# A long convolution beside a gated feed-forward layer: one outer transform table for all residues, phase factors in the inner tables

## The chip, the cores and the metric

The kernel runs on one core of one Trainium2 chip. The metric is the time on the device in microseconds (us). A core has a matrix engine (TensorE; PE in the profile, PEld for its weight loads), VectorE (DVE), ScalarE (ACT), GpSimd (POOL) and SyncE (SP), which here issues nearly all DMAs. The engines run beside one another and wait for each other through semaphores.

## What is computed

With S = 2048 positions and D = 640 channels, bf16 in and out:

```python
xn = layernorm(A_q)                                  # over D, no scale, no shift
k_shift[s] = sum_m A_k[s - m] * shift_k[:, m]        # 4 taps
kv = k_shift * A_v
y = irfft(rfft(kv, 4096) * rfft(ssm_k, 4096))[:2048] + kv * ssm_D   # causal convolution, length 2048
h = sigmoid(xn @ w_gate) * (xn @ w_up)               # 640 -> 1728
out = A_q + xn * y + h @ w_down                      # 1728 -> 640
```

## The kernel before

Position s is written 16 p + b, with p the partition (0 to 127) and b the residue (0 to 15); all activations lie in SBUF as [p, b, channel]. Two streams of work share the engines.

The **feed-forward stream** goes through four groups t of 512 positions. xnT holds the transposed xn of a group. For each of 13 column blocks fc of 128, `product` (L284 to L290) makes five matmuls of 128x512 for the gate and five for the up weights; `gate_ev` puts the gate through a sigmoid on ScalarE (L297) and `up_ev` multiplies on VectorE (L303); a fourteenth block (L309) holds the last 64 columns of both. `down_mm` (L332) then makes for each of four position blocks two halves of 320 columns out of 14 matmuls each, in two parts of seven, and `down_ev` (L337) adds them to x.

The **convolution stream** goes through five chunks c of 128 channels. `kv_op` builds kv on VectorE (L365 to L374), and `h_turn` (L351) brings in the filter, so that `kvh` holds kv and the filter side by side. The transform has 128 frequency rows k1 (real and imaginary part) times 16 inner frequencies. It has four steps on PE:

- `st1_mm` (L391, L393): the outer transform over p. For each residue b and each half (cosine, sine) one 128x128 table of S1 is the stationary operand, with 128 columns of kv and 128 of the filter as moving operands. S1 has 32 such tables, because the phase of residue b is in it. A block n has four residues, that is eight matmuls of 128 columns. `st1_ev` brings the block to SBUF, `wr1` (L405) writes it to a DRAM tensor d1, and `rd2` (L415) reads it back with frequency row k1 = 4 r + q split so that q, the half and the residue are on the partitions.
- `st2_mm` (L424): the inner transform over the 16 residues, as 32x32 matmuls. PE is used as 4 x 4 tiles of 32 rows and 32 columns; tile (q, g) takes the data of rows q and two values of r at a time, 512 columns, and all of them have the same weights, SM[:, 0]. A step s has 16 such matmuls; there are 20 steps. `st2_ev` brings the result to `xz`.
- `prod` (L437, L439) multiplies the two spectra on VectorE. `inv1_mm` (L453) goes back over the inner frequencies: two sets of weights (i = 0, 1, accumulated) times 16 tiles, 512 columns each, 32 matmuls for each of 10 steps y. `inv1_ev` and `wr2` (L469, L473) write to a DRAM tensor d2, and `rdb` (L483) reads it back.
- `inv2_mm` (L492): the outer transform back, with TB (again one table for each residue), eight matmuls of 128 columns for each of 20 blocks. `inv2_q` and `inv2_x` (L497, L502) multiply with xn and add to x.

The copies from PSUM that are written `copy` in these helpers run on ScalarE (recorded as L251) or on VectorE (L254).

**Order.** Nothing is scheduled automatically. Each kind of step has a letter and a list (`chains`, L560 to L668), and a string ORDER (L670) says letter by letter which list gives the next step; each engine then runs its instructions in that order. Capital F, I and J are the evictions B, A and C put on VectorE. TURNS gives the order within the loads (m) and the stores (o).

**Prologue** (L505 to L557). Position blocks 0 to 3 of x are loaded, two by SP and ACT together and two by one each; then come gate and up weights for the first 128 columns (gate by SP, up by ACT), for the next 128, and for columns 256 to 511 (SP). Thirteen matmuls on zeros (L522, `busy`) keep PE running meanwhile. The layer norm of blocks 0, 1 and 3 uses VectorE's bn_stats (L205), aggregate (L209) and variance (L238), then POOL's power (L242) and VectorE's xn (L247). That of block 2 uses two ScalarE passes over x with accumulated sums (`ln_sums`, L215 and L216), VectorE's L222, the same power, and L233. `turn(i)` transposes block i on PE (L261) and copies it to xnT on ScalarE (L264). In between, as FIRST says, `quarter` makes the products of fc 0 and 1 for one position block at a time (L279, 128 columns): g00 is the gate of fc 0 for block 0, t1 is `turn(1)`.

Of the kernel before, what the change touches and what calls it, by code (L numbers as in the profile page):

```python
# [17 lines left out]
DM = 640  # L18
# [8 lines left out]
g00 t1 u00 t2 g10 u10 t3 g01 u01 g11 u11 g02 u02 g12 u12 g03 u03 g13 u13  # L27
# [3 lines left out]
def _bf16_bits(a):  # L31
    a = np.ascontiguousarray(a, dtype=np.float32)
    u = a.view(np.uint32)
    r = (u + 0x7FFF + ((u >> 16) & 1)) & 0xFFFF0000
    return (r >> 16).astype(np.uint16)


def _tables():

    p = np.arange(P)
    k1 = p + 0.25
    s1 = np.zeros((P, NB, 2, P))
# [4 lines left out]
    tb = s1.transpose(3, 2, 1, 0) / 2048.0  # L50
    th = 2 * np.pi * np.outer(np.arange(NB), np.arange(NB)) / 16.0
    c, s = np.cos(th), np.sin(th)
    s2 = np.block([[c, -s], [s, c]])
    a1 = np.block([[c.T, s.T], [-c.T, -s.T]])
    a2 = np.block([[-s.T, c.T], [-s.T, c.T]])
    small = np.stack([s2, a1, a2], 1)
    return _bf16_bits(s1), _bf16_bits(tb), _bf16_bits(np.concatenate([small] * NQ, 0))
# [3 lines left out]
def kernel(  # L61
# [23 lines left out]
    s1bits, tbbits, smbits = _tables()  # L85
# [3 lines left out]
    SMd = nc.inline_tensor(smbits, name="tabSM")  # L89
# [16 lines left out]
    SM = SMt.bitcast(BF16)  # L106
# [111 lines left out]

    def ln_sums_var(g, i):

        d = lns[g]
        nc.vector.tensor_scalar(d["var"][:, i:i + 1], d["ss"][:, i:i + 1], 1.0 / DM, 1e-5, op0=ALU.mult, op1=ALU.add)  # L222
# [116 lines left out]
    def store(b0, b1, lo, hi):  # L339
        sync.dma_start(outr[:, b0:b1, lo:hi], x[:, b0:b1, lo:hi])  # L340
# [37 lines left out]
    def quad(i):  # L378
        return slice(32 * i, 32 * i + 32)
# [38 lines left out]
    def st2_mm(s):  # L418

        d = groups[s]  # L420
        d["ps"] = ps = [psC.tile([P, 2, 2, 2, P], F32, name="ps2", tag="c") for _ in range(2)]
        for g in range(4):
            for q in range(NQ):
                nc.tensor.matmul(ps[q // 2][quad(g), q % 2, :, :, :], lhsT=SM[quad(q), 0, :],  # L424
                                 rhs=d["t2"][quad(q), 2 * g:2 * g + 2, :], start=True, stop=True)
# [16 lines left out]
    def inv1_mm(y):  # L442

        c, y2 = divmod(y, 2)
        d = chunks[c]
        if y2 == 0:
            d["d2"] = dr.tile([32, P, P], BF16, name="d2", bufs=NC)
        d["pa", y] = ps = [psC.tile([P, 2, 512], F32, name="psa", tag="c") for _ in range(2)]
        lo, hi = sorted((2 * y % 3, (2 * y + 1) % 3))
        for i in range(2):  # L450
            for q in range(NQ):
                for g in range(4):
                    nc.tensor.matmul(ps[g // 2][quad(q), g % 2, :], lhsT=SM[quad(g), 1 + i, :],  # L453
                                     rhs=xz[quad(g), lo:hi + 1:hi - lo, 1 + i, 2 * q:2 * q + 2, :],
                                     start=(i == 0), stop=(i == 1))
# [30 lines left out]
    def inv2_mm(c, m):  # L486

        bi = chunks[c]["bi", m // 2]
        chunks[c]["pb", m] = ps = psG.tile([P, 4, P], F32, name="psb", tag="g")
        for i in range(4):  # L490
            for h in range(2):
                nc.tensor.matmul(ps[:, i, :], lhsT=TB[:, h, 4 * m + i, :], rhs=bi[:, h, 4 * (m % 2) + i, :],  # L492
                                 start=(h == 0), stop=(h == 1))
# [30 lines left out]
    def turn(i):  # L524
        xn_mm(i)
        xn_ev(i)
# [10 lines left out]
    ln_sums(0, 2)  # L537
# [42 lines left out]
    def hs(c):  # L580
        return [(load_h, c)]
# [7 lines left out]
    for k in ((load_w, sync, 512, 768, 0),  # L589
              (load_w, sync, 512, 768, 1),  # L590
              (load_taps, 0),
              (sync.dma_start, SMt[:], SMd.ap()),
# [11 lines left out]
              (sync.dma_start, S1t[:], S1d.ap()),  # L604
              *hs(1),
# [4 lines left out]
    for k in ((load_x, sync, 2), (load_x, sync, 3), (sync.dma_start, TBt[:], TBd.ap())):  # L610
        step("n", *k)
# [53 lines left out]
    for b in range(12, NB - 1):  # L665
# [5 lines left out]
    mmgmmgsummggggsmsugmmgmgLsuuLsZgLkkggskkmggmmuusggnkLsmuLugsPmkmgumgHgggsLusguggllsuggguHggummgggkmL  # L671
    mLlmDkaaTkkkluAgkkkueAeekggggktkkekkuaaHgukAmAgsawAakgAPgsuuHlmkuKgmkkkTagskkKwwauAAggDkkgKaashtukkk
    AkAggkgwmwsuslauaAAHgklgkkuVVskaaAAggaksgkkkwAaAggrbuugkkkwsuBBgpkKrHpDasATaAtkugsKnguwwbKBgKFgasgAa
    AggasuskkpkkVkahwAnrLAwLgguugkpHHgaaAkAgggDcukCJLggeealuALuaIwggbrkeBBgggeurkkkVTuukkKkubggBBgbBgBpw
    rgppkasupaAIuggstkkkukVwkWaAaAhskgugPaAarkpggAcksJCggbwsuuHHKggDBWlpgBrassupukakggpAAsbBBgggkucwkRss
    VkkCJggbBupupdqggrrqBspWsbupgguBdBcskrJCgqgbggkFRBusubgFllpBwgaAudaggaAWdarrqqgpAAlgwpppeauqRagAIuqq
    egeecJCuuggubFpBpWpggbrrggBBuudqdcCJwwgqpgsRWgqpbFBpggsuurbBBprpggssugucdJCWdgpbsgqFBgubBBpqsgpgspuc
    rCgJgspqqubgugqRdBBdrbWpqqgpgsugqqBBpcCJprsuggbsuBBRdqWpgsdRRpgggsqqucuJCgggWsqduqqdqggudquqdRRooggg
    gqoggoooqqududugqqqguqooddqqqqgggougoouooo
    """  # L680
    TURNS = {"m": [1, 7, 4, 9, 21, 0, 20, 2, 10, 5, 6, 13, 12, 14, 8, 17, 15, 11, 22, 18, 16, 19, 23, 25, 24, 3],
        "o": [2, 0, 4, 1, 5, 3, 7, 6, 8, 11, 10, 9, 12, 13]}
# [35 lines left out]
```

## Time and profile before

| | |
|---|---|
| median of 3 runs | 236.09 us (235.89 to 236.45) |
| profiled execution | 236.47 us, of which the span of its instructions is 234.5 us |
| PE clock granted | 1.00 throughout |
| matmuls and weight loads | 2201 of each |
| L288 (gate and up products) | 500 matmuls of 512 columns |
| L391, L393 (outer transform) | 320 matmuls of 128 columns |
| L492 (outer transform back) | 160 matmuls of 128 columns |
| L424, L453 (inner, 32x32) | 320 and 320 matmuls of 512 columns |
| DMA | 56.78 MB, of it S1t and TBt 1024 KB each, SMt 24 KB |

A row of the profile's table of groups gives line, engine and operation, what is written and read with the shape, how often, then busy time and mean length, and last how long the engine had stood idle before and what ended that. A row of a timeline gives start, length, engine, line, operation, shape, and in brackets the idle time before it with its cause. The end of a matmul is modelled: a 512-column matmul is recorded as 380 ns long, but the next one starts 216 ns after it, so the pace is read from starts. The waits of an engine are listed as total time, times, and the longest.

### The profile page before, as it was taken

What the parts mean: (1) busy time and instruction counts of PE and PEld (TensorE: products, weight loads), DVE (VectorE), ACT (ScalarE), POOL (GpSimd) and SP (SyncE); (2) the same over time, 40 slices, a digit from 0 to 9 for tenths busy, and PEclk for the clock granted to TensorE, in tenths of its full rate; (3) what the DMA queues carried; (4) which work ended last, traced back from release to release, by engine and by line L of the source; (5) the groups of instructions that cost most, each with busy time, mean ns of one, the idle gap of its engine ahead of it and who ended that gap; (6) DMA issues with size and microseconds to landing.
All of it is one profiled execution on the core that took longest, in us unless ns stands there. A gap on an engine that the chain in (4) does not pass through costs nothing. (4 is left out here: it accounts for less than half of the span.)

```text
span 234.5 us, 5457 instructions
## 1 busy us (share of the span) xinstructions
PE 227.0 (97%) x2201; PEld 130.8 (56%) x2201; DVE 198.5 (85%) x327; ACT 136.3 (58%) x199; POOL 12.1 (5%) x27
## 2 busy tenths in 40 slices
PE   6799999999999999999999999999999999999994
PEld 2664445777556555766554534478554435356772
DVE  4433764899999999969999999999999999998673
ACT  2737777346578696977776876564365666652000
POOL 5301020200001000003000000000000000000000
PEclk9999999999999999999999999999999999999999
DMA  6999999879959998999997997999899898376675
GB/s 168 272 283 279 290 338 226 260 141 253 313 186 232 301 309 219 309 253 295 256 230 178 280 301 185 276 254 246 188 288 294 205 268 209 115 163 197 220 240 169
DMA packets 98926, 56.78 MB, mean 242 GB/s; under 512 B 58518, under 2 KB 93142, under 8 KB 98646
## 3 DMA queue, kind: packets, MB, share of 16 engines
q1 hardware_dynamic: 97814, 55.95, 89.4%
q10 hardware_dynamic: 1088, 0.49, 0.9%
q8 instruction: 17, 0.28, 0.5%
q14 instruction: 7, 0.06, 0.1%
HBM read 36.12 MB, written 18.35 MB: 232 GB/s over the span
## 5 line engine op out<-in xcount | busy, mean ns | idle before, releaser
L288 PEld LDWEIGHTS <-w 128*128 128x128 bf16 x500 | 46.5, 98 | 54.8 <-issue 5.0
L332 PE MATMUL pd<-wd,hT 128*128 128x320 bf16 (+2 forms) x448 | 64.5, 299 | 0.0
L288 PE MATMUL pu<-xnT,w 128*128 128x512 bf16 x250 | 62.3, 380 | 0.0
L288 PE MATMUL pg<-xnT,w 128*128 128x512 bf16 x250 | 62.2, 379 | 0.0
L332 PEld LDWEIGHTS <-hT 128*128 128x128 bf16 x448 | 42.1, 98 | 18.7 <-issue 2.1
L303 DVE TENSOR_TENSOR hT<-sig,pu 128x512 bf16<-128x512 bf16 x52 | 34.7, 680 | 15.2 <-PE pu L288 11.1
L251 ACT CAST t<-ps 128x1024 bf16<-128x1024 f32 x37 | 36.0, 1013 | 18.7 <-PE ps L393 16.0
L251 ACT CAST xz<-ps 128x1024 bf16<-128x1024 f32 x34 | 33.0, 1015 | 17.8 <-PE ps L424 17.8
L297 ACT ACTIVATE sig<-pg 128x512 bf16<-128x512 f32 x52 | 30.8, 602 | 20.7 <-PE pg L288 15.1
L439 DVE TENSOR_TENSOR xz<-xz 128x2048 bf16<-128x2048 bf16 x20 | 24.3, 1216 | 0.1
L371 DVE TENSOR_TENSOR acc<-acc,tmp 128x1024 bf16<-128x1024 bf16 x30 | 20.6, 688 | 0.5
L369 DVE TENSOR_TENSOR tmp<-kx,sc 128x1024 bf16<-128x1024 bf16 x30 | 20.6, 686 | 0.5
L393 PE MATMUL ps<-kvh,S1t 128*128 128x128 bf16 x160 | 20.8, 219 | 0.0
L391 PE MATMUL ps<-kvh,S1t 128*128 128x128 bf16 x160 | 20.8, 218 | 0.0
L337 DVE TENSOR_TENSOR x<-pd,x 128x320 bf16<-128x320 f32 (+2 forms) x32 | 14.9, 481 | 5.3 <-PE pd L332 5.2
L391 PEld LDWEIGHTS <-S1t 128*128 128x128 bf16 x160 | 15.5, 97 | 2.2
L393 PEld LDWEIGHTS <-S1t 128*128 128x128 bf16 x160 | 15.4, 96 | 2.2
L497 DVE TENSOR_TENSOR yx<-psb,xn 128x512 bf16<-128x512 f32 x20 | 13.7, 686 | 1.7 <-PE psb L492 0.9
L437 DVE STREAM_SHUFFLE xz<-xz 128x512 f32<-128x512 f32 x20 | 14.5, 724 | 0.0
L251 ACT CAST ao<-psa 128x1024 bf16<-128x1024 f32 x8 | 8.1, 1012 | 8.9 <-PE psa L453 8.8
L215 ACT ACTIVATE xn<-x 128x640 bf16<-128x640 bf16 x13 | 9.5, 732 | 3.5 <-DMA x<-in_A_q_dram 3.5
L254 DVE CAST ao<-psa 128x1024 bf16<-128x1024 f32 x8 | 9.8, 1222 | 2.0 <-PE psa L453 1.9
(55 smaller groups left out, 168.4 us busy)
## 6 DMA issues: line engine op xcount, KB each, us to landing
d<-t SPq DMA_DIRECT2D x20, 512.0 KB, 4.7
t<-d SPq DMA_DIRECT2D x20, 512.0 KB, 6.1
bi<-d SPq DMA_DIRECT2D x8, 512.0 KB, 6.5
d<-ao SPq DMA_DIRECT2D x6, 512.0 KB, 6.5
kx<-in_A_k_dram SPq DMA_DIRECT2D x10, 256.0 KB, 4.9
hn<-in_A_ssm_k_dram SPq DMA_DIRECT2D x20, 128.0 KB, 4.0
kvh<-in_A_v_dram SPq DMA_DIRECT2D x10, 256.0 KB, 5.1
x<-in_A_q_dram SPq DMA_DIRECT2D x3, 640.0 KB, 7.2
```

The source lines that it names most:

```text
L251: nc.scalar.copy(out=out, in_=in_)
L288: nc.tensor.matmul(pg[:, :], lhsT=w[:, c, u * UP + fc * P:u * UP + (fc + 1) * P], rhs=xnT[:, :, c, :], start=(c == 0), stop=(c == NC - 1))
L297: nc.scalar.activation(sig[fc][:, :], pgs[0, fc][:, :], ACT.Sigmoid)
L303: nc.vector.tensor_tensor(hT[:, fc, :], sig[fc][:, :], pgs[1, fc][:, :], ALU.mult)
L332: nc.tensor.matmul(pd[:, :], lhsT=hT[:, fc, bb * P:(bb + 1) * P], rhs=wd[:, fc, es], start=(fc == 0), stop=(fc == NFC - 1))
L337: nc.vector.tensor_tensor(x[:, 4 * t + bb, es], pds[bb, half][:, :], x[:, 4 * t + bb, es], ALU.add)
L369: nc.vector.tensor_tensor(d["tmp"][:, :, :], kx[:, lo + 3 - m:hi + 3 - m, :], sb(m), ALU.mult)
L371: nc.vector.tensor_tensor(d["acc"][:, :, :], d["acc"][:, :, :], d["tmp"][:, :, :], ALU.add)
L391: nc.tensor.matmul(ps[:, i, 0:P], lhsT=S1[:, b, h, :], rhs=cin[c]["kvh"][:, 0, b, :], start=True, stop=True)
L393: nc.tensor.matmul(ps[:, i, P:2 * P], lhsT=S1[:, b, h, :], rhs=hp[:, b // 2, b % 2, :], start=True, stop=True)
L437: nc.vector.stream_shuffle(z[:, 2, :, :].bitcast(F32), z[:, 1, :, :].bitcast(F32), swap)
L439: nc.vector.tensor_tensor(z[:, 1:3, :, :], z[:, 0:1, :, :].to_broadcast((P, 2, 8, P)), z[:, 1:3, :, :], ALU.mult)
```

## The change

- **Outer tables.** S1 and TB keep only the table of residue 0 (two of 128x128 each). The phase 2 pi k1 b / 2048 of residue b, which depends on the frequency row, moves into the inner weights: FW has a 32x32 matrix for each of the 128 frequency rows (forward), IW two for each (back).
- **`st1_mm`, `inv2_mm`.** Since all residues have the same stationary operand, a block is two matmuls of 512 columns in place of eight of 128. `st1_ev` puts the result back in the old order of d1.
- **`st2_mm`, `inv1_mm`.** A frequency row has its own weights, so the moving operand is cut: a forward step has 32 matmuls of 256 columns, in two passes over the 16 tiles; a step back has 128 matmuls of 128 columns, in eight passes.
- **Prologue.** Block 2 takes its statistics on VectorE like the others. The first weights come as one load of 256 columns for the gate and one for the up weights, both by SP. FIRST has a new order.
- **Order.** ORDER and TURNS are new strings, with the same steps (S1t, FWt, IWt, TBt in place of S1t, SMt, TBt among the loads). Evictions on VectorE: six of `st2_ev` as before, seven of `st1_ev` for three, seven of `inv1_ev` for ten.
- **Last store.** The one of the last 128 columns is issued by ScalarE.

The lines of ORDER and the table functions are cut here.

```diff
-g00 t1 u00 t2 g10 u10 t3 g01 u01 g11 u11 g02 u02 g12 u12 g03 u03 g13 u13
+g00 g10 t1 u00 u10 t2 g01 g11 u01 u11 t3 g02 u02 g12 u12 g03 u03 g13 u13
...
-    S1t = res.tile([P, NB, 2, P], U16, name="S1t")
-    TBt = res.tile([P, 2, NB, P], U16, name="TBt")
-    SMt = res.tile([P, 3, 32], U16, name="SMt")
+    S1t = res.tile([P, 2, P], U16, name="S1t")
+    TBt = res.tile([P, 2, P], U16, name="TBt")
+    IWt = res.tile([P, 2, 32, 32], U16, name="IWt")
+    FWt = res.tile([P, 32, 32], U16, name="FWt")
...
-        sync.dma_start(outr[:, b0:b1, lo:hi], x[:, b0:b1, lo:hi])
+        (nc.scalar if b1 == NB and hi == DM else sync).dma_start(outr[:, b0:b1, lo:hi], x[:, b0:b1, lo:hi])
...
-        pss[n] = ps = psC.tile([P, 4, 2 * P], F32, name="ps1", tag="c")
-        for i in range(4):
-            b = 4 * n4 + i
-            nc.tensor.matmul(ps[:, i, 0:P], lhsT=S1[:, b, h, :], rhs=cin[c]["kvh"][:, 0, b, :], start=True, stop=True)
-            hp = cin[c]["kvh"][:, 1, :, :].rearrange("p b c -> p (b c)").rearrange("p (b c e) -> p b e c", b=8, e=2)
-            nc.tensor.matmul(ps[:, i, P:2 * P], lhsT=S1[:, b, h, :], rhs=hp[:, b // 2, b % 2, :], start=True, stop=True)
+        pss[n] = ps = psC.tile([P, 2, 4, P], F32, name="ps1", tag="c")
+        hp = cin[c]["kvh"][:, 1, :, :].rearrange("p b c -> p (b c)").rearrange("p (b c e) -> p b e c", b=8, e=2)
+        nc.tensor.matmul(ps[:, 0, :, :], lhsT=S1[:, h, :], rhs=cin[c]["kvh"][:, 0, 4 * n4:4 * n4 + 4, :],
+                         start=True, stop=True)
+        nc.tensor.matmul(ps[:, 1, :, :], lhsT=S1[:, h, :], rhs=hp[:, 2 * n4:2 * n4 + 2, :, :], start=True, stop=True)
...
-        copy(out=d[n // 2][:, o:o + 4, :, :].rearrange("p b s c -> p b (s c)"), in_=pss[n][:, :, :])
+        copy(out=d[n // 2][:, o:o + 4, :, :].rearrange("p b s c -> p s b c"), in_=pss[n][:, :, :, :])
...
-        for g in range(4):
-            for q in range(NQ):
-                nc.tensor.matmul(ps[q // 2][quad(g), q % 2, :, :, :], lhsT=SM[quad(q), 0, :],
-                                 rhs=d["t2"][quad(q), 2 * g:2 * g + 2, :], start=True, stop=True)
+        for e in range(2):
+            for g in range(4):
+                for q in range(NQ):
+                    nc.tensor.matmul(ps[q // 2][quad(g), q % 2, e, :, :], lhsT=FW[quad(q), 8 * (s % 4) + 2 * g + e, :],
+                                     rhs=d["t2"][quad(q), 2 * g + e, :], start=True, stop=True)
...
-        for i in range(2):
-            for q in range(NQ):
-                for g in range(4):
-                    nc.tensor.matmul(ps[g // 2][quad(q), g % 2, :], lhsT=SM[quad(g), 1 + i, :],
-                                     rhs=xz[quad(g), lo:hi + 1:hi - lo, 1 + i, 2 * q:2 * q + 2, :],
-                                     start=(i == 0), stop=(i == 1))
+        for k in range(2):
+            s = 2 * y + (k if lo == 2 * y % 3 else 1 - k)
+            for e in range(2):
+                j = 8 * (s % 4) + 4 * e
+                o = (2 * k + e) * P
+                for i in range(2):
+                    for q in range(NQ):
+                        for g in range(4):
+                            nc.tensor.matmul(ps[g // 2][quad(q), g % 2, o:o + P], lhsT=IW[quad(g), i, j + q, :],
+                                             rhs=xz[quad(g), s % 3, 1 + i, 2 * q + e, :],
+                                             start=(i == 0), stop=(i == 1))
...
-        for i in range(4):
-            for h in range(2):
-                nc.tensor.matmul(ps[:, i, :], lhsT=TB[:, h, 4 * m + i, :], rhs=bi[:, h, 4 * (m % 2) + i, :],
-                                 start=(h == 0), stop=(h == 1))
+        for h in range(2):
+            nc.tensor.matmul(ps[:, :, :], lhsT=TB[:, h, :], rhs=bi[:, h, 4 * (m % 2):4 * (m % 2) + 4, :],
+                             start=(h == 0), stop=(h == 1))
...
-        load_w((sync, nc.scalar)[u], 0, P, u)
-    for u in range(2):
-        load_w(sync, P, 256, u)
+        load_w(sync, 0, 256, u)
...
-    ln_sums(0, 2)
     ln_stats(0, 1)
     ln_xn(0, 0)
     ln_ready(0, 1)
     turn(0)
+    ln_stats(0, 2)
+    ln_xn(0, 1)
+    ln_ready(0, 2)
     ln_stats(0, 3)
-    ln_sums_var(0, 2)
-    ln_pow(0, 2, 3)
-    ln_xn(0, 1)
+    ln_xn(0, 2)
     ln_ready(0, 3)
-    ln_sums_xn(0, 2)
     ln_xn(0, 3)
...
-              (sync.dma_start, SMt[:], SMd.ap()),
...
+              (sync.dma_start, FWt[:], FWd.ap()),
...
-    for k in ((load_x, sync, 2), (load_x, sync, 3), (sync.dma_start, TBt[:], TBd.ap())):
+    for k in ((load_x, sync, 2), (load_x, sync, 3), (sync.dma_start, IWt[:], IWd.ap()),
+              (sync.dma_start, TBt[:], TBd.ap())):
```

More of the change, by code (lines that the diff above doesn't have):

```diff
@@ L49, in _tables @@
         s1[:, b, 1, :] = -np.sin(psi)
-    tb = s1.transpose(3, 2, 1, 0) / 2048.0
+    tb = s1[:, 0].transpose(2, 1, 0) / 2048.0
     th = 2 * np.pi * np.outer(np.arange(NB), np.arange(NB)) / 16.0
[L52 to L57, printed above, removed]
+    iw = np.zeros((4, 32, 2, 4, 2, NQ, 32))
+    for g in range(4):
+        for s4 in range(4):
+            for e in range(2):
+                for q in range(NQ):
+                    ph = th + 2 * np.pi * k1[4 * (8 * s4 + 2 * g + e) + q] * np.arange(NB)[None, :] / 2048.0
+                    ci, si = np.cos(ph), np.sin(ph)
+                    iw[g, :, 0, s4, e, q, :] = np.block([[ci, si], [-ci, -si]])
+                    iw[g, :, 1, s4, e, q, :] = np.block([[-si, ci], [-si, ci]])
+    fw = np.zeros((NQ, 32, 32, 32))
+    for q in range(NQ):
+        for r in range(32):
+            ph = th + 2 * np.pi * k1[4 * r + q] * np.arange(NB)[:, None] / 2048.0
+            fw[q, :, r, :] = np.block([[np.cos(ph), -np.sin(ph)], [np.sin(ph), np.cos(ph)]])
+    return (_bf16_bits(s1[:, 0]), _bf16_bits(tb), _bf16_bits(iw.reshape(P, 2, 32, 32)),
+            _bf16_bits(fw.reshape(P, 32, 32)))
 @with_exitstack
@@ L83 @@
     Drow = A_ssm_D.rearrange("(o d) -> o d", o=1)
[L85 removed]
+    s1bits, tbbits, iwbits, fwbits = _tables()
     srow = A_shift_k.rearrange("d m -> (d m)").rearrange("(o n) -> o n", o=1)
@@ L421, in st2_mm @@
         d["ps"] = ps = [psC.tile([P, 2, 2, 2, P], F32, name="ps2", tag="c") for _ in range(2)]
-        for g in range(4):
-            for q in range(NQ):
-                nc.tensor.matmul(ps[q // 2][quad(g), q % 2, :, :, :], lhsT=SM[quad(q), 0, :],
-                                 rhs=d["t2"][quad(q), 2 * g:2 * g + 2, :], start=True, stop=True)
+        for e in range(2):
+            for g in range(4):
+                for q in range(NQ):
+                    nc.tensor.matmul(ps[q // 2][quad(g), q % 2, e, :, :], lhsT=FW[quad(q), 8 * (s % 4) + 2 * g + e, :],
+                                     rhs=d["t2"][quad(q), 2 * g + e, :], start=True, stop=True)
     def st2_ev(s, n, copy=act_copy):
```

34 lines of the change are left out of this document (18 added, 16 removed).

## Prediction

> **What bounds the kernel now.** I read the page's busy shares first, then the waits of PE, then the busy time by stage, and last the timelines of the prologue, of one transform stage and of the end.
>
> ```profile
> PE 227.0 (97%) x2201; PEld 130.8 (56%) x2201; DVE 198.5 (85%) x327; ACT 136.3 (58%) x199; POOL 12.1 (5%) x27
> ```
> ```profile
> PE pg L279 <- ACT xnT L264: 1.7, 1, 1.7
> PE idle L522 <- DVE hT L120: 1.2, 1, 1.2
> PE pt L261 <- DVE xn L247: 0.7, 1, 0.7
> PE psa L453 <- DVE xz L437: 0.6, 1, 0.6
> ```
>
> The second view says more than the first: PE waits four times in all, three of them before 8.53 us, and no wait names a DMA. From 8.53 us to its last matmul at 231.2 us PE stands still for 0.57 us. So the time is the first 8.5 us, PE's own work, and the 3.2 us behind it. By stage VectorE is nearly as full: busy 39.3 of 40 us between 50 and 90 us, 37.3 between 90 and 130 and 38.7 between 130 and 170, so it has 4.7 us to spare in 120.
>
> Prologue, columns start, length, engine, line:
>
> ```profile
> 6.12 0.74 ACT L215 ACTIVATE xn<-x 128x640 bf16<-128x640 bf16 x1 [3.46 <-DMA x<-in_A_q_dram]
> ...
> 7.81 0.67 ACT L264 COPY xnT<-pt 128x640 bf16<-128x640 bf16 x1
> ```
> ```profile
> 5.69 0.45 PE L261 MATMUL pt<-ident,xn 128*128 128x128 bf16 x5 [0.69 <-DVE xn L247]
> ...
> 8.53 0.44 PE L279 MATMUL pg<-xnT,w 128*128 128x128 bf16 x5 [1.74 <-ACT xnT L264]
> ```
> ```profile
> 6.95 0.10 PEld L279 LDWEIGHTS <-w 128*128 128x128 bf16 x1 [0.65 <-DMA w<-in_B_w_gate_dram]
> ```
>
> The first transposes are done at about 6.15 us, but their copy (L264) stands behind ScalarE's two statistics passes over x (L215, L216; 6.12 to 7.9 us), so the first product starts at 8.53, though its weights were there at 6.95.
>
> Transform, the small blocks (32x32 tiles) and the 128-column blocks:
>
> ```profile
> 128.56 0.43 PE L424 MATMUL ps<-t,SMt 32*32 32x512 bf16 x16
> ```
> ```profile
> 173.17 0.65 PE L453 MATMUL psa<-xz,SMt 32*32 32x512 bf16 x32
> ```
> ```profile
> 191.99 0.20 PEld L453 LDWEIGHTS <-SMt 32*32 32x32 bf16 x31 [0.55 <-issue]
> ```
> ```profile
> 172.35 0.89 PE psb L492 x16
> ```
>
> Sixteen tile matmuls take 0.43 us and 32 take 0.65: a second round of 16 tiles adds 0.22 us, which is what one 512-column matmul of full size takes (five in 1.08 us in the chain). So the 16 tiles stream at the same time, and the rest of a block is fixed. From a block's start to the next start it is 0.58 us for 32 and 0.37 for 16, so about 0.15 us beyond the rounds. The third line is what the change hangs on: 31 weight loads of 0.088 us each start within 0.20 us, (0.20 - 0.09)/30 = 3.7 ns apart, with the first round's matmuls between them.
>
> **Part by part.** *Outer transforms (L391, L393, L492).* Forty blocks of eight 128-column matmuls and twenty of the same on the way back become blocks of two 512-column ones. The columns stay the same (1024), so only the joints go. 16 in 0.89 us is 0.445 for a block; the sixteen of L391 and L393 that run from 132.17 to 133.08 us give 0.455. Two of 512 take 2 x 0.216 = 0.432. I take 0.02 less for each of 60 blocks, **-1.0 us** (-0.8 to -1.4). The weight loads that go (480 full ones become 120) run beside matmuls and free no time by themselves.
>
> *Forward inner blocks (L424).* 16 x 512 columns become 32 x 256: two rounds of 0.11 us for one of 0.22, with the second round's loads in the shadow of the first. **0** (0 to +0.2 over 20 blocks).
>
> *Backward inner blocks (L453).* 32 matmuls of 512 columns become 128 of 128, ten times: eight rounds of 16, each with new weights. A round needs 0.056 us (the 128-column pace) and 16 issues of 3.7 ns need 0.059, so the two are level: 8 x 0.059 + 0.15 = 0.62 for 0.58, **+0.4 us** in all. No row shows more than 32 such pairs in a row, nor a tile reloaded every 0.056 us, so I bound it. Below, 8 x 0.054 + 0.15 = 0.58 makes it nothing. Above, from two rows: if a load's 0.088 us is bare in every round, 8 x 0.144 + 0.15 = 1.30, or +7.2 us in all; if pairs come only at the pace of the full-size 128-column runs (0.056 a pair), 128 x 0.056 + 0.15 = 7.3, or +67 us. I stay near the low end, because its row is the same instruction on the same tiles.
>
> The Trainium skill, TensorE: Matmul & The Clock Gate, section "Wait — 56ns, not 53.3ns?", speaks against this edit: matmuls never start closer than about 25 ns however few columns they have. By it a block would take an estimated 128 x 25 ns = 3.2 us and the ten +27 us. The row of 31 loads in 0.20 us does not bear it out across different tiles.
>
> *Prologue.* ScalarE's passes for block 2 go; VectorE does bn_stats for it. ScalarE then copies xnT at 6.2 to 6.9 us. The gate weights now come as one 256-column load, 320 KB for 160 first; by the second 160 KB load of before, which landed at about 7.6, I put its landing at 7.5, and g00 there. VectorE by the rows (statistics 0.89, aggregate, variance and their gaps 0.6, POOL power 0.56, xn 0.45): xn of block 1 starts at 7.0 (8.00 now), of block 2 at 8.6 (8.88), of block 3 at 10.0 (9.41). PE: g00 g10 to 8.1, t1 to 8.35, u00 u10 once the up weights land at about 8.7 (both up loads of before were in by 8.9), t2 and four quarters to 10.65, t3 to 10.95 (xn of block 3 is there at 10.45), eight quarters to 13.2. Now it is 13.87: **-0.65 us**. The bounds are -1.0 (20 quarters and three transposes back to back from 7.5) and 0 (weights only at 8.5). Its new bound is VectorE's third xn, 0.2 us ahead of its use.
>
> *Loads.* Tables shrink from 2072 KB (S1t, TBt, SMt) to 896 KB, and the last store goes out on ScalarE's queue. No PE wait names a DMA; the forward reads of d1 land 0.7 to 4 us ahead of their blocks and the last read of d2 2.6 us ahead, so bytes saved are worth **0**. Should that cover fail, the shortest, 0.7 us, is gone first. At the end the last addition ends at 231.55, SP issues the store at 231.83 behind another one; issued by ScalarE at about 231.6 it lands **0.2 us** earlier.
>
> *Order and evictions.* The hand-written order is new. VectorE takes 20 evictions for 19 (1.22 us each, against 1.01 on ScalarE), so 1.2 us more in a stage with 4.7 spare: **0**, and +1.2 if that spare lies elsewhere.
>
> Sum: -1.0 + 0 + 0.4 - 0.65 - 0.2 = -1.45 us. The profiled execution took 236.47 (span 234.46, 2.0 around it), so 235.0; it lies 0.4 above the median of 236.09, where the same sum gives **234.7**.
>
> **Rivals.**
> 1. *Supply of the small matmuls bounds (slower).* 128 pairs are four times the longest run shown, and each block pays if its instructions come slower than they ran from a filled queue. It decides from 4.8 ns a pair: the other terms give 1.85 us, 0.185 a block, and (0.58 + 0.185 - 0.15)/128 = 4.8. At 56 ns a pair the time is 302. For: only bursts of 32 pairs are shown, and they had piled up behind a wait. Against: no break in them. By the Trainium skill's 25 ns (same section) it would be an estimated 262. Chance 0.08.
> 2. *Bare weight loads.* Each round shows its 0.088 us: 241.5. For: 32-column loads last nearly as long as a round is now short. Against: first-round matmuls last 385 ns and those with weights already in 372, so a bare load costs 13 ns. Chance 0.10.
> 3. *The new order leaves PE waiting for VectorE*, as at 191.4 us (0.57 us for a shuffle). Three such waits, 1.5 us or so: 236.2 (235.5 to 237.5). For: VectorE at 96% from 50 to 170 us, one more eviction. Against: four waits in the whole trace of before. Chance 0.20.
> 4. *The prologue does not do what it says*: weights in one larger load arrive at 8.5, and the start does not move: 235.3. Chance 0.10.
>
> **How the numbers follow.** The forecast, 234.7 (its own range 234.1 to 235.4), has 0.52. A measurement of this kernel can tell about 0.2%, 0.47 us, so faster is below 235.6 and slower above 236.6. Faster: 0.50 of the forecast and 0.07 of rival 4, 0.57. Same: 0.02, 0.03 and 0.11 of rival 3, 0.16. Slower: 0.09 of rival 3 and rivals 1 and 2, 0.27. The range leaves out rivals 1 and 2 (0.18) and reaches over rival 3: 233.8 to 237.6.
>
> **What would show it.** Backward blocks of 128 at 0.6 us from start to next start (over 0.75 the gain is gone; 1.3 is rival 2; over 2 is rival 1); outer blocks at 0.43; first product at about 7.5 and first 512-column product at 13.2; PE without waits after that. New rows of PE waiting for VectorE, or a first product that names the weight DMA beyond 8 us, would make the forecast wrong.

## The result: 251.3 us, slower by 6.5%

| | before | after |
|---|---|---|
| median of 4 runs each, in turn | 236.2 us | 251.3 us (250.9 to 253.0) |
| after / before | | 1.065, 95% interval 1.060 to 1.070 |
| profiled execution / its span | 236.47 / 234.5 us | 252.97 / 250.8 us |
| first 512-column product starts | 13.87 us | 12.55 us |
| backward inner block, start to next start | 0.583 us | 1.198 us |
| last matmul starts | 231.00 us | 246.70 us |
| from there to the end | 3.5 us | 4.1 us |

Single executions of three kernels below ran with PE at about half of its pace (h1, 393 us) or a sixth (b128 and p, 1325 us each) from start to end; they are left out of the times, and so are the profiles taken from them (the first of h1, the only one of p).

The page of the changed kernel (busy time, granted clock by slices of 6.27 us, and the DMA queue that carries instructions):

```profile
PE 238.7 (95%) x3121; PEld 126.6 (50%) x3121; DVE 202.4 (81%) x331; ACT 134.1 (53%) x194; POOL 12.1 (5%) x27
...
PEclk9999999999999999999999999998895999999999
...
q8 instruction: 24, 0.39, 0.7%
```

PE is the bound still, with 11.7 us more of busy time, though the columns are the same; VectorE's share has fallen to 81%. The clock, 1.00 throughout before, dips in slices 27, 28 and 30 (counted from 0). The last row is of a kind that the prediction did not use: q8 moves 24 pieces of 16 KB (17 before). The trace has 6242 matmuls and weight loads of PE, 260 for each piece, and 4402 before, 259 for each: so I take these to be PE's own instructions, 256 to a piece.

PE's waits, total, times and longest:

```profile
PE ps L432 <- issue: 5.5, 2, 3.6
PE pd L340 <- issue: 1.2, 1, 1.2
PE idle L532 <- DVE hT L133: 1.2, 1, 1.2
PE pg L296 <- DVE hT L311: 0.2, 1, 0.2
```

Of the forecast's rivals, waiting for VectorE has 0.2 us. What is new is "issue": PE waits for nothing that the profile shows, three times, 6.7 us. One backward block, and the stretch around the longest of these waits (columns as before):

```profile
136.07 1.26 PE L466 MATMUL psa<-xz,IWt 32*32 32x128 bf16 x128
137.27 0.82 PE L296 MATMUL pg<-xnT,w 128*128 128x512 bf16 x3
```
```profile
184.96 0.32 PE L432 MATMUL ps<-t,FWt 32*32 32x256 bf16 x14
188.84 0.61 PE L432 MATMUL ps<-t,FWt 32*32 32x256 bf16 x18 [3.56 <-issue]
189.38 2.31 PE L296 MATMUL pu<-xnT,w 128*128 128x512 bf16 x5
191.48 1.91 PE L504 MATMUL psb<-bi,TBt 128*128 128x512 bf16 x4
```

The first fence: 1.20 us from block to product. Inside it, by the starts in the trace, the matmuls of the first 32 pairs of weight load and matmul start within 0.12 us, then none until 0.25, and from there every pair starts 8.33 ns after the one before, without any mark of the rounds of 16: 0.25 + 95 x 8.33 ns, and 0.15 from the last pair to the product, are the 1.20 us. The second fence: a forward block stops after 14 of its 32 matmuls and goes on 3.8 us later. Behind it the five matmuls of one product take 2.1 us from start to next start; at full clock five take 1.08.

The three pauses have a place in common. Counted along PE's stream (weight loads, matmuls and the 14 records of its sequencer, from 1), the first instruction behind each is record 3266, 3778 and 4290: 512 apart, that is two pieces. And each time a piece of q8 had landed 1.3 to 1.5 us before PE went on (153.14 and 154.42 us, 170.68 and 172.19, 187.43 and 188.84). So my theory after the profile: **the backward blocks run at the pace at which PE is given instructions, 8.3 ns a pair once its queue of 32 pairs is empty; and since such a block uses up a whole piece of 256 in 1.2 us, PE arrives at pieces that have not been fetched yet, and stands still.** The rivals: every round shows its weight loads (the forecast's rival 2, whose 1.30 us is near the 1.20 measured), and the pauses belong to the forward blocks, the new order or a buffer.

### The profile page after: what moved, and what is told of

Read it like the earlier page. It is cut to its first block, busy times and chain, and to the rows that moved or that the text cites. A ratio compares the mean times of both kernels' runs of the same rounds, so it can differ in the third digit from the quotient of the medians.

```text
span 250.8 us, 7290 instructions
## 1 busy us (share of the span) xinstructions
PE 238.7 (95%) x3121; PEld 126.6 (50%) x3121; DVE 202.4 (81%) x331; ACT 134.1 (53%) x194; POOL 12.1 (5%) x27
## 4 chain that ended last, share of the span: by engine, by line
PE 93%; issue 4%; DVE 1%; ACT 0%; DVEq 0%
PE pd L340 25%; PE pu L296 22%; PE pg L296 22%; PE psa L466 5%; PE psb L504 4%; PE ps L400 3%; PE ps L432 3%; PE ps L398 3%; PE pg L317 2%; PE idle L532 2%; PE pg L287 1%; PE pu L287 1%; PE pt L269 1%; DVE hT L311 0%; ACT xnT L272 0%
## 5 line engine op out<-in xcount | busy, mean ns | idle before, releaser
L340 PE MATMUL pd<-wd,hT 128*128 128x320 bf16 (+2 forms) x448 | 66.8, 303 | 1.2 <-issue 1.2
L296 PE MATMUL pu<-xnT,w 128*128 128x512 bf16 x250 | 63.3, 385 | 0.0
L340 PEld LDWEIGHTS <-hT 128*128 128x128 bf16 x448 | 43.2, 99 | 23.9 <-issue 2.6
L259 ACT CAST t<-ps 128x1024 bf16<-128x1024 f32 x33 | 32.5, 1011 | 21.2 <-PE ps L400 19.7
L345 DVE TENSOR_TENSOR x<-pd,x 128x320 bf16<-128x320 f32 (+2 forms) x32 | 14.9, 482 | 6.0 <-PE pd L340 5.8
L259 ACT CAST ao<-psa 128x1024 bf16<-128x1024 f32 x11 | 10.8, 1014 | 13.3 <-PE psa L466 10.5
L400 PE MATMUL ps<-kvh,S1t 128*128 128x512 bf16 x40 | 15.5, 388 | 0.0
L398 PE MATMUL ps<-kvh,S1t 128*128 128x512 bf16 x40 | 15.2, 379 | 0.0
L432 PE MATMUL ps<-t,FWt 32*32 32x256 bf16 x640 | 9.8, 283 | 5.5 <-issue 5.5
L466 PEld LDWEIGHTS <-IWt 32*32 32x32 bf16 x1280 | 10.8, 88 | 4.4 <-issue 3.5
L466 PE MATMUL psa<-xz,IWt 32*32 32x128 bf16 x1280 | 12.7, 222 | 0.0
L262 DVE CAST xz<-ps 128x1024 bf16<-128x1024 f32 x6 | 7.4, 1225 | 5.2 <-PE ps L432 4.9
```

What stands on the lines that cost most here:

```text
L259: nc.scalar.copy(out=out, in_=in_)
L296: nc.tensor.matmul(pg[:, :], lhsT=w[:, c, u * UP + fc * P:u * UP + (fc + 1) * P], rhs=xnT[:, :, c, :], start=(c == 0), stop=(c == NC - 1))
L340: nc.tensor.matmul(pd[:, :], lhsT=hT[:, fc, bb * P:(bb + 1) * P], rhs=wd[:, fc, es], start=(fc == 0), stop=(fc == NFC - 1))
L398: nc.tensor.matmul(ps[:, 0, :, :], lhsT=S1[:, h, :], rhs=cin[c]["kvh"][:, 0, 4 * n4:4 * n4 + 4, :], start=True, stop=True)
L400: nc.tensor.matmul(ps[:, 1, :, :], lhsT=S1[:, h, :], rhs=hp[:, 2 * n4:2 * n4 + 2, :, :], start=True, stop=True)
L432: nc.tensor.matmul(ps[q // 2][quad(g), q % 2, e, :, :], lhsT=FW[quad(q), 8 * (s % 4) + 2 * g + e, :], rhs=d["t2"][quad(q), 2 * g + e, :], ...
```

## Experiments on the way back and the pauses

**The change without its way back, and without its way forward.** Kernel h1 is the changed kernel with `inv1_mm` and `inv2_mm` as before (the fence has the matmul of `inv1_mm` alone):

```diff
...
-                            nc.tensor.matmul(ps[g // 2][quad(q), g % 2, o:o + P], lhsT=IW[quad(g), i, j + q, :],
-                                             rhs=xz[quad(g), s % 3, 1 + i, 2 * q + e, :],
...
+                    nc.tensor.matmul(ps[g // 2][quad(q), g % 2, :], lhsT=IW[quad(g), i, :],
+                                     rhs=xz[quad(g), lo:hi + 1:hi - lo, 1 + i, 2 * q:2 * q + 2, :],
...
```

> The changed kernel with the old way back (one inverse table for all rows, full outer table, 32 inner matmuls of 512 columns a block, eight outer ones of 128); the way forward, the loads, the prologue and the order stay new. Theory (what is lost is lost in the backward inner blocks: their 128 pairs run at the pace at which PE's instructions are supplied, 8.3 ns a pair after the first 32, and they use up the 256 instructions of a fetched piece in 1.2 us, so that PE later stands still for 7.5 us behind a late fetch): blocks at 0.58 us again, no idle time of PE over 0.6 us in the second half, the prologue's 1.3 us gained, in all 234.0 to 235.2. Rival A (the forward blocks of 32 pairs or the new order make the long pauses, which stood before forward blocks): pauses of 2 to 4 us stay, 240 to 243. Rival B (the fetches stay late whatever the blocks, because of what the other queues do): as A.

Kernel h2 is the changed kernel with `st1_mm` and `st2_mm` as before.

> The changed kernel with the old way forward (S1 table of 16 residues, 128-column outer matmuls, 16 inner matmuls of 512 columns a block); the way back, the loads, the prologue and the order stay new. Theory (backward inner blocks at the pace of supply, with late fetches behind them): backward blocks at 1.20 us, that is +6.1 us in ten, 236.2 - 1.3 + 6.1 = 241 if no pause of PE falls in, and up to 4 us for each pause of PE that does; the places of the pauses move, since the 256-instruction pieces begin elsewhere: 241 to 250. Rival (the forward blocks make the pauses): 241 with no idle time over 1 us, and the other kernel of this call, with the old way back, keeps them.

h1 took 236.96 us, 1.001 of before (0.999 to 1.004); h2 251.64 (247.9 to 254.6, four runs). A second execution of h1, for its profile (the expectation is further down), has blocks of 0.583 us and no pause on issue at all, while its forward blocks of 32 pairs stand there unchanged, at 0.370 us. h2 has the pauses without the new forward blocks: 2.5 us before a product at 131 us, and 0.8 us within a backward block. So the way back makes both losses. That h1 would gain 1.3 us was wrong; the next section is about that.

**The count alone.** b128 is the kernel before, with its 32 backward matmuls cut into 128, weights, order and everything else as they were:

```diff
...
-                    nc.tensor.matmul(ps[g // 2][quad(q), g % 2, :], lhsT=SM[quad(g), 1 + i, :],
-                                     rhs=xz[quad(g), lo:hi + 1:hi - lo, 1 + i, 2 * q:2 * q + 2, :],
...
+                            nc.tensor.matmul(ps[g // 2][quad(q), g % 2, o:o + P], lhsT=SM[quad(g), 1 + i, :],
+                                             rhs=xz[quad(g), (lo, hi)[k], 1 + i, 2 * q + e, :],
...
```

> The kernel before with one edit: the 32 backward inner matmuls of 512 columns of a block cut into 128 of 128 columns, with the old weights and in the order that the change uses; columns, prologue, forward way, loads and order of the work stay as before. Theory (the count of instructions alone makes the loss): blocks of 1.20 us for 0.58, +6.2 us in ten, and PE's pauses of 1 to 4 us behind late fetches with a few us of lower clock after them, in all 242 to 254, and the larger part of the change's loss is here. Rival A (it needs the new weights, one set for every frequency row, or the new forward blocks and order as well): blocks of 1.20 us but no pauses, 242 to 243. Rival B (weight loads of the tiles, as theirs is the same set again and again): blocks of 1.2 to 1.3 us, no pauses, 242 to 243.

247.9 us, 1.044 of before (1.037 to 1.050). Its waits and the rows of its longest pause:

```profile
PE ps L424 <- issue: 2.1, 1, 2.1
...
PE pg L288 <- issue: 1.1, 1, 1.1
```
```profile
129.66 0.41 PE L424 MATMUL ps<-t,SMt 32*32 32x512 bf16 x10
132.19 0.40 PE L424 MATMUL ps<-t,SMt 32*32 32x512 bf16 x6 [2.10 <-issue]
132.52 2.08 PE L288 MATMUL pu<-xnT,w 128*128 128x512 bf16 x5
```

Blocks of 1.199 us in the median (four of the ten take 1.24 to 1.53), pauses on issue at 129.7 and 193.9 us (records 2498 and 4802), and half clock behind the first. A block of 16 pairs, which has nothing new in it, is what stands still: the bill for a dense block comes at a later piece, wherever that begins. Rivals A and B are out.

**Half the cut.** b64 is the same with 64 matmuls of 256 columns.

> The kernel before with the 32 backward inner matmuls of 512 columns of a block cut into 64 of 256 columns, old weights. Theory (supply: a queue of 32 pairs, then 8.3 ns a pair): the last pair starts at 0.25 + 32 x 8.3 ns = 0.52 us, 0.16 us behind it to the next start, 0.67 us a block for 0.58, and 128 instructions a block are too few in a row for a late fetch: +0.9 us in all, 236.5 to 237.5, no new pauses of PE. Rival (a bare weight load of 88 ns in every round): 4 x (0.088 + 0.107) + 0.15 = 0.93 us a block, 239.5. Rival (the formula of the forecast, four rounds at the pace of the columns and 0.15): 0.58, no change.

Blocks of 0.770 us; 237.4 us, 1.0035 of before (1.0006 to 1.0065), no pause on issue. The count of the queue is right, the size of the block was not: the 33rd pair starts at 0.305 us, not 0.25 (the second round, still out of the queue, starts 0.12 us behind the first, probably since it waits for the 256 columns of that), 31 pairs of 8.35 ns follow, and the last one is 0.21 us ahead of the next start, not 0.16. Bare weight loads (0.93) and the forecast's formula (0.58) are both further off. Of the 1.9 us that ten blocks lose, 0.6 is paid by a wait of before that is gone (L453 for VectorE).

**The pace by itself.** m1 is the kernel before with a probe behind its last product, beside which no engine works. `tiles(r, where, n)` makes r rounds of matmuls of n columns over the 32x32 tiles in `where` (`every` is all 16), `full(r, n)` makes r on the whole array, and `spacer` 28 of 512 columns:

```diff
+    spacer(); tiles(8, every, 128)
+    spacer(); tiles(8, every, 32)
+    spacer(); tiles(32, [(i, i) for i in range(4)], 32)
+    spacer(); full(128, 32)
+    spacer(); tiles(32, every, 32)
+    spacer()
```

> The kernel before, with a probe on PE behind its last product (its results go nowhere): runs of pairs of weight load and matmul, each run behind 28 matmuls of 512 columns that let the queue fill: 128 pairs over 16 tiles with 128 columns; the same with 32 columns; 128 pairs over four tiles (the diagonal) with 32 columns; 128 pairs of full 128x128 size with 32 columns; 512 pairs over 16 tiles with 32 columns. Theory (supply of instructions): behind the first 32 pairs all three runs of tiles go at about 8.3 ns a pair, whatever the columns and however many tiles share them: 0.12 + 96 x 8.3 ns = 0.9 us for each; the run of 512 pairs needs four fetched pieces of 256 instructions and goes slower than 8.3 ns a pair in the mean, with pauses. Rival (each tile is busy for its weight load of 88 ns and its columns before its next pair): 16 tiles with 128 columns 8.3 to 9 ns, with 32 columns about 6.3 ns, four tiles with 32 columns about 25 ns a pair. The Trainium skill (TensorE: Matmul & The Clock Gate, section 'Wait - 56ns, not 53.3ns?') would have 25 ns a pair in all of them as a floor.

```profile
239.28 1.27 PE L699 MATMUL prb<-hT 32*32 32x128 bf16 x128
...
246.63 1.19 PE L699 MATMUL prb<-hT 32*32 32x32 bf16 x128
...
253.89 1.19 PE L699 MATMUL prb<-hT 32*32 32x32 bf16 x128
...
261.06 3.35 PE L704 MATMUL gap<-hT 128*128 128x32 bf16 x128
...
270.40 1.64 PE L699 MATMUL prb<-hT 32*32 32x32 bf16 x182
274.19 1.22 PE L699 MATMUL prb<-hT 32*32 32x32 bf16 x128 [2.15 <-issue]
277.64 1.22 PE L699 MATMUL prb<-hT 32*32 32x32 bf16 x128 [2.23 <-issue]
281.37 0.77 PE L699 MATMUL prb<-hT 32*32 32x32 bf16 x74 [2.51 <-issue]
```

This timeline of the probe settles the pace. With 128 columns over 16 tiles, with 32 over 16, and with 32 over four tiles, 128 pairs start within 1.04, 1.00 and 1.01 us, and in each the pairs from the 41st on are 8.33 ns apart. Neither the columns nor the number of tiles that share the loads changes that number, and out of a filled queue pairs of the same kind start 3 to 4 ns apart over 16 tiles; so it is the supply. Full-size pairs are 25.0 ns apart. The Trainium skill, TensorE: Matmul & The Clock Gate, section "Wait — 56ns, not 53.3ns?", gives that 25 ns as what starts never drop below; this trace agrees for the full array, and not across different tiles, where starts are 8.3 ns apart and 3 to 4 ns out of a filled queue. The 64 instructions that start in a burst agree with the queue of 64 in the same page (section "Architectural detail: the array is 16× 32×32, not 1× 128×128").

The last four rows show the second loss without a kernel around it: a pause of 2.3 to 2.7 us (start to start) every 128 pairs, which is every 256 instructions. Without any other traffic PE cannot do better than one piece in about 3.5 us: pieces were fetched at 271.84, 275.30, 278.78 and 282.52 us, each taking 1.1 to 1.4 us. From 273.2 us on the granted clock is 0.50 there; m2, below, has 3.4 to 3.5 us for a round of 264 instructions at 1.00 throughout.

**How thin is thin enough.** m2 has the same bursts of 128 pairs, each with N matmuls of 512 columns behind it.

```diff
+    for count in (4, 8, 12, 16):
+        spacer(40)
+        for _ in range(5):
+            tiles(8, every, 128)
+            spacer(count)
```

> The kernel before, with a second probe behind its last product: bursts of 128 pairs of weight load and matmul over 16 tiles (256 instructions, 128 columns, as a backward block of the change), each followed by N matmuls of 512 columns, five times for each N of 4, 8, 12 and 16; 40 such matmuls ahead of each set. No other engine works there. Theory (a piece of 256 instructions comes every 3.5 us at best, as 128 pairs did in the long run of the first probe, 1.0 us of work and 2.3 to 2.7 us of pause): a round of 256 + 2N instructions takes its own time, 1.2 us + N x 0.216 us, or 3.5 us x (256 + 2N)/256, whichever is longer, once the pieces fetched ahead are used: with N = 4 2.1 us of work and up to 3.6 us a round, with 8 2.9 and 3.7, with 12 3.8 and 3.8 (no pause over 0.5 us), with 16 4.7 and no pause. Rival (pauses belong to the long unbroken run of small pairs alone): no pauses with any N.

```profile
242.50 0.30 PE L699 MATMUL prb<-hT 32*32 32x128 bf16 x22
243.93 1.08 PE L699 MATMUL prb<-hT 32*32 32x128 bf16 x106 [1.13 <-issue]
...
245.91 0.28 PE L699 MATMUL prb<-hT 32*32 32x128 bf16 x18
247.38 1.12 PE L699 MATMUL prb<-hT 32*32 32x128 bf16 x110 [1.19 <-issue]
```

The break moves by four pairs from round to round (22 then 106, 18 then 110), since a round has 264 instructions and a piece 256. Times from burst to burst, start to start:

| N | instructions | own time (1.2 + N x 0.216) | measured, us |
|---|---|---|---|
| 4 | 264 | 2.1 | 2.17, 3.41, 3.49, 3.49 |
| 8 | 272 | 2.9 | 3.03, 3.42, 4.07, 3.79 |
| 12 | 280 | 3.8 | 3.89, 3.89, 3.89, 3.89 |
| 16 | 288 | 4.7 | 4.76, 4.75, 4.76, 5.77 |

The break-even is where it was expected, at about 3.5 us for 256 instructions. One thing was not: the last round of N = 16 has a pause of 1.0 us, though the stream is thin enough. The piece landed at 335.2 us, 1.4 us before PE went on; its fetch had begun late. What decides when a fetch begins is not shown by any run here.

**The pauses moved by 60 instructions.** sh is the changed kernel with ten of its idle matmuls at the start cut into forty:

```diff
-        for _ in range(n):
-            nc.tensor.matmul(idle[:, :], lhsT=hT[:, 0, 0:P], rhs=hT[:, 0, :], start=True, stop=True)
+        k = 4 if n == 10 else 1
+        for _ in range(k * n):
+            nc.tensor.matmul(idle[:, 0:512 // k], lhsT=hT[:, 0, 0:P], rhs=hT[:, 0, 0:512 // k], start=True, stop=True)
```

> The changed kernel with its ten idle 512-column products ahead of the first transposes cut into forty of 128 columns: the same columns, 60 more instructions of PE (30 weight loads and 30 matmuls), all before 4 us. Nothing else is changed. Theory (the pauses come where the stream crosses from one fetched piece of 256 instructions into the next while the fetch is late): backward blocks stay at 1.20 us, and the pauses at 152.9, 170.0 and 185.0 us go to other places in the stream, 60 instructions earlier in the program's order, or change in length; the time may come out some us off 251.3 either way (244 to 254). Rival (the pauses belong to these instructions: a buffer, a semaphore, a DMA that they wait for): the same pauses before the same instructions, 251.3 within 0.5.

251.4 us, 1.062 of before (1.055 to 1.068), as the change itself. The long pauses are at 138.8 us (ahead of a product), 154.9 and 197.2 us (within forward blocks); none of the three old ones is left. The profile puts the first down to ScalarE, the copy that had last released something:

```profile
PE ps L432 <- issue: 4.8, 2, 2.4
PE pg L296 <- ACT ao L259: 1.8, 1, 1.8
```

The count of the stream shows that it is of the same kind as the others:

```
kernel          first record behind each long pause      that number modulo 256
the change      3266, 3778, 4290                         194, 194, 194
sh              2754, 3266, 4802                         194, 194, 194
h2              2498, 5058                               194, 194
b128            2498, 4802                               194, 194
m1              6082, 6338, 6594                         194, 194, 194
```

Ten pauses in four programs, before four kinds of instruction, and three in the probe, all at one point of a piece; in the ten PE goes on 1.3 to 1.6 us after a piece has landed. The rival, that these instructions wait for something of their own, is out.

## Experiments on the gain that was left

The prologue gives 1.3 us, and h1, which has it and none of the losses above, is no faster than before. Kernel p is before with the changed prologue alone (FIRST, too, is the changed one; the fence leaves it out):

```diff
-        load_w((sync, nc.scalar)[u], 0, P, u)
-    for u in range(2):
-        load_w(sync, P, 256, u)
+        load_w(sync, 0, 256, u)
...
-    ln_sums(0, 2)
...
+    ln_stats(0, 2)
...
-    ln_sums_xn(0, 2)
+    ln_xn(0, 2)
```

> The kernel before with the changed kernel's prologue alone (statistics of all four blocks on VectorE, first weights in one load of 256 columns, the first quarters and transposes in the new turn); transforms, tables, loads behind it and the order of the work as before. Theory (the prologue brings the first 512-column product 1.3 us forward, and nothing behind it takes that back): 234.6 to 235.3. Rival (an earlier start is eaten by what bounds the later stages, VectorE at 96% from 50 to 170 us or TensorE's granted clock): 235.8 to 236.6, the first product 1.3 us earlier all the same.

Kernel pf adds the new way forward to it, in the old order.

> The kernel before with the changed prologue and the new way forward (one outer table, 512-column outer matmuls, 32 inner matmuls of 256 columns, tables for every row), in the old order of loads and work, with the old way back. Theory: outer blocks 0.443 us for 0.455, forty of them -0.5 us; inner forward blocks 0.370 for 0.367, twenty of them +0.1; so 0.4 less than the prologue alone, 234.8 to 235.1, and no pause of PE. Rival (32 pairs in a forward block use up instructions fast enough for late fetches): pauses of 1 us and more, 236 to 240.

And h1 once more, for its profile:

> The changed kernel with the old way back once more, for a profile at full clock, since the first profiled execution ran with TensorE at half its clock throughout. Theory: backward blocks at 0.58 us, first 512-column product at 12.5 us, no pause of PE over 0.6 us from 140 us on; the 1.3 us of the prologue and the 0.3 us of the outer transforms must then be lost in waits of PE for VectorE under the new order (rows of PE waiting for DVE of 1 to 2 us in all) or in a granted clock below 1.00 (0.5% of clock is 1.2 us). Rival: pauses of PE in front of forward blocks are still there, smaller.

p took 235.4 us, 0.995 of before (0.992 to 0.998), a little over the upper end expected; pf 235.35, 0.996 (0.994 to 0.998), also a little over; the gain of the forward part (blocks of 0.443 us for 0.455) is too small for these runs to show, which cannot tell p and pf apart. Both beat the kernel before, by 0.4 to 0.5%. In pf's profile the first 512-column product starts at 12.77 us, 1.1 earlier than before. So the prologue's gain is real in the old order, and h1 does not have it in the new one. Its second profile (of an execution of 238.2 us, 1.3 above h1's median) shows two losses, a wait and the end (windows: from, to, length, busy time of each engine, granted clock, DMA share, GB/s):

```profile
PE pd L335 <- DMA wd<-in_B_w_down_dram: 1.7, 1, 1.7
```
```profile
226.00:231.00 5.00, 5.00 (x48) 3.23 (x46) 3.74 (x8) 0.00 (x0) 0.00 (x0) 1.00 0.57 164
231.00:236.10 5.10, 0.25 (x5) 0.08 (x2) 0.49 (x2) 0.00 (x0) 0.00 (x0) 0.76 0.70 239
```

The same windows of the kernel before:

```profile
226.00:231.00 5.00, 5.00 (x48) 3.23 (x46) 3.73 (x8) 0.00 (x0) 0.00 (x0) 1.00 0.46 122
231.00:234.50 3.50, 0.22 (x4) 0.04 (x1) 0.46 (x2) 0.00 (x0) 0.00 (x0) 1.00 0.49 164
```

First, PE comes to the first down product earlier (37.5 us in h1, 38.7 before), and SP issues the second part of its weights at 30.6 us, 26.2 before. Second, behind the last matmul h1 still has 239 GB/s x 5.1 us = 1.2 MB to move, the kernel before 0.57 MB. Three kernels tried to take these away. hw puts the two loads of the down weights next to each other in their list again; a load of x from another list still comes between them, and the second part is issued at 27.8 us:

```diff
-    TURNS = {"m": [1, 9, 0, 2, 8, 20, 4, 3, 13, 6, 5, 11, 12, 21, 10, 7, 17, 16, 14, 19, 15, 22, 23, 24, 25, 18],
+    TURNS = {"m": [1, 9, 0, 2, 8, 20, 4, 3, 13, 6, 5, 11, 12, 7, 16, 21, 10, 17, 14, 19, 15, 22, 23, 24, 25, 18],
```

> The changed kernel with the old way back, and with the two loads of the down weights issued one behind the other and ahead of three other loads, as before the change. Theory (with the old way back the start that is 1.3 us earlier is lost again at the first down product, where PE waits 1.7 us for the second part of the down weights, since the new order issues it at 30.6 us for 26.2): the wait goes or falls under 0.5 us, and the time is 1.0 to 1.7 us less than with the old way back alone: 235.0 to 235.9. Rival (the wait only hides a bound that shows elsewhere, VectorE or the clock): the wait goes and the time stays at 236.5 to 237.

hs gives the stores of the last four blocks to ScalarE; pb does the same to pf:

```diff
-        (nc.scalar if b1 == NB and hi == DM else sync).dma_start(outr[:, b0:b1, lo:hi], x[:, b0:b1, lo:hi])
+        (nc.scalar if b0 >= 12 else sync).dma_start(outr[:, b0:b1, lo:hi], x[:, b0:b1, lo:hi])
```

> The changed kernel with the old way back, and with the five stores of blocks 12 to 15 issued by ScalarE, which has nothing left to do by then, for SP (the change gives it the last one alone). Theory (under the new order SP's stores pile up: one issue stands 1.6 us at 227.7 us, the next six follow it without a break until 233.2, and the end comes 5.1 us behind the last matmul for 3.5 before): 3.5 to 4.1 us behind the last matmul, 1.0 to 1.5 us less than with the old way back alone: 235.3 to 236.0. Rival (the writes themselves, not their issue, are late, since DMA is what is full): the stores are issued earlier, land no earlier, and the time stays at 236.5 to 237.

> The kernel before with the changed prologue and the new way forward (as in the run that had those two in the old order), and the five stores of blocks 12 to 15 issued by ScalarE. Theory: there SP's stores pile up less, the end is 3.65 us behind the last matmul; the last store is issued 0.2 us earlier: 235.1 to 235.3. Rival (the writes are what is late): 235.35 again within 0.1.

hw: 238.1 us, 1.0045 of before (1.001 to 1.008). The wait is gone and the time is no better: the last matmul starts 0.5 us earlier than in h1, and the end comes 5.5 us behind it. hs: 237.5, 1.003 (1.000 to 1.006); in its profile the wait did not occur and the last matmul starts at 229.6 us, 1.4 earlier than before, yet the end comes 5.4 us behind it, again with 1.2 MB left. pb: 235.7, 0.998 (0.995 to 1.000), no gain over pf; in its profile the end comes 3.4 us behind the last matmul for pf's 3.7, but the last matmul is 0.9 us later. So none of the three changes of issue gained time. In hs the stores have another queue and the end is no nearer to the last matmul, which points at the bytes there, not at their queue. The new order leaves twice the bytes for the end. Which of its moves does that was not tried.

## Why the prediction failed, step by step

**Backward inner blocks (+0.4 us): the step that failed.** The term was mis-sized: 0.62 us a block was forecast, 1.198 measured, +6.15 us in ten. The pace of 3.7 ns was read from 31 loads that had piled up behind a wait, and I wrote myself that they had; "no break in them" was no evidence, since 32 pairs are just what the queue holds. Rival 1 had the mechanism and the right break-even, 4.8 ns a pair; the supply gives 8.3. It got 0.08 because its prices (56 and 25 ns) were those of full-size matmuls. Rival 2's 1.30 us was near by chance: its loads are in none of the probe's numbers. By the prediction's own signs (1.3 is rival 2, over 2 is rival 1) 1.198 would have been read as rival 2.

**What no term and no rival had.** Late fetches: the three pauses come to 7.4 us (1.35, 2.2 and 3.8 by starts, less the pace). The clock behind them: the granted clock is 0.50 from 173.6 to 177.0 and from 187.2 to 194.0 us, and where PE works in these stretches (from 188.8 in the second) matmuls start 427 ns apart (512 columns) or 267 (320), half pace; by the starts that costs 1.7 and 2.3 us, 4.0 in all.

```profile
186.00:189.00 3.00, 0.17 (x16) 0.16 (x17) 0.00 (x0) 0.00 (x0) 0.00 (x0) 0.70 1.10 332
189.30:192.80 3.50, 3.50 (x11) 1.16 (x9) 2.23 (x3) 1.01 (x1) 0.00 (x0) 0.50 0.62 171
```

These windows of the changed kernel (granted clock third from the end) show it: half clock in the stretch behind the pause, and already in a part of the pause.

**Outer transforms (-1.0).** 0.443 for 0.455 us and 0.432 for 0.447: -0.8 us, the mechanism right, the size a little less (the prediction's own 0.02 for 60 blocks would be -1.2, not -1.0; it was 0.012 and 0.015). **Forward inner blocks (0).** 0.370 for 0.367: right.

**Prologue (-0.65).** First product at 7.13 us (7.5 forecast), first 512-column product at 12.55 (13.2 forecast): -1.3, outside its bounds (-1.0 to 0). The mechanism was right, the size too small: the weights came earlier than put, and so did VectorE's xn of blocks 1 to 3 (6.60, 8.04 and 9.44 us for 7.0, 8.6 and 10.0), so that PE goes without a break from 7.13 us. **Loads (0)** and **last store (-0.2).** The forecast looked for cover in the transforms and not at the down weights, whose cover is what the earlier start takes away; the wait shows in h1, in h2 (1.9 us) and in sh (0.9), not in the profiled execution of the change. The last store is issued by ScalarE as forecast, but SP's store before it is later, and the end is 0.6 us longer. **Order and evictions (0), rival 3.** Waits of PE for VectorE are 0.2 us: right, the rival did not come.

The sum by starts: -1.3 + 6.15 + 7.4 + 4.0 - 0.8 + 0.05, less the 0.6 of the wait of before (L453 for VectorE) that is gone, is 14.9 us of the 15.7 by which the last matmul is later; 0.8 us is not assigned. With 0.6 at the end that is the span's 16.3. This is the profiled execution, of 252.97 us and a mean granted clock of 0.980; the other three (250.9 to 251.5 us) have 0.993, which makes their clock term an estimated 1.7 us ((1 - 0.993) x 249).

## What to carry over

A pace read from a burst behind a wait is that of the queue's content: before it is multiplied, ask how many instructions the row had and whether the new run is longer. Here a run of tile matmuls of 32, 128 or 256 columns goes at 8.3 ns a pair beyond 32 pairs, and a stretch that uses 256 instructions of PE in less than about 3.5 us can pay again later, at a place that any edit ahead of it moves. Cutting matmuls to save full-size weight loads is worth only the joints (0.012 to 0.015 us a block); count the instructions that the other side of the trade adds.

## What was not expected of the hardware

- PE's instructions come in pieces of 256 over a DMA queue of their own, and PE goes on 1.2 to 1.6 us after a late piece has landed; the pauses were 0.6 to 3.8 us.
- The clock can halve behind pauses of two to four microseconds. The granted clock was 0.50 for 3.4 us at the change's pause of 2.2 us, for 6.8 us at its pause of 3.8 us, and for 3.4 us at one pause each in sh (2.7 us), h2 (2.9) and b128 (2.5), but not at those of 2.0 and 2.6 us in sh. It began between 1.6 us before PE went on and 1.4 us after. The Trainium skill, TensorE: Matmul & The Clock Gate, section "HAM oscillation — how this bites in real kernels", warns of gaps over about 3.4 us; four of these five pauses were shorter. In m1, with three pauses of 2.3 to 2.7 us in a row, the half clock lasted 13.7 us.
